# A fused gated-attention and gated-MLP kernel: the first four chunks issued in a searched unit order, and the first halves of two output products summed by way of SBUF

## The chip, the cores and the metric

The kernel runs on one core of a Trainium2 chip. The metric is the device time of one launch in microseconds (us), lower is better. A run's time is about 1.8 us longer than the span of its profile, which goes from the first to the last instruction.

Names: PE is the matrix engine, PEld its weight loads, DVE VectorE, ACT ScalarE, POOL GpSimd, SPq the queue that issues DMA loads. In this program PE's products are written to tiles in PSUM, and all other tiles lie in SBUF; an eviction copies a result out of PSUM. The granted clock is the share of its full speed at which PE ran, by the profile.

## The reference, cut to what matters

```python
# q, k, v, alpha: (4, 8, 768, 48) float32
state = alpha_t[..., None] * state + outer(k_t, v_t)     # per head, over 768 steps
y_t   = q_t @ state
x     = y, heads joined: (3072, 384)
h     = x @ w_in            # (384, 2048)
g     = h * cos(h)
out   = g @ w_out           # (2048, 384)
```

The kernel cuts the 3072 rows into 24 chunks of 128. For a chunk it takes logarithms of alpha, sums them by a triangular product, exponentiates, scales q and k, transposes them, forms masked scores, and carries a state to the next chunk. Then come the first product (ff1, in two halves of 24 products of 128 columns), the cosine on ScalarE, the gating on VectorE, and the second product (ff2, two halves of 8 products of 384 columns).

## The kernel before: the parts that matter here

The program is scheduled by hand. In these traces each engine takes its instructions in the order in which they were issued, also where a later one is ready sooner. So the order of the units is the schedule.

```python
def cast_w2(f):                       # fp32 -> bf16, one half of w_out
    nc.vector.tensor_copy(out=w2[:, f : f + 5], in_=w2f[:, f : f + 5])
    nc.scalar.activation(out=w2[:, f + 5 : f + 8], in_=w2f[:, f + 5 : f + 8], func=AF.Copy)

def ff2(j, half):
    if half == 0:
        o_new = ps.tile([C, 512], FP, tag="o")      # one PSUM buffer only
        o_ps[j] = o_new
    for f in range(HF):
        ft = half * HF + f
        nc.tensor.matmul(o_ps[j][:, 0:DM], g_t[j][:, ft], w2[:, ft],
                         start=(ft == 0), stop=(ft == NF - 1))

def ev_ff2(j):
    o_sb = moe.tile([C, DM], FP, tag="o_sb", bufs=3)
    nc.scalar.activation(out=o_sb, in_=o_ps.pop(j)[:, 0:DM], func=AF.Copy)
    ...

def warmup(n):                        # products on zeros, nobody reads them
    w_ps = ps.tile([C, 512], FP, tag="o")
    for _ in range(n):
        nc.tensor.matmul(w_ps, warm[:, 0:C], warm, start=True, stop=True)
...
for s in range(NCH + 2):              # step s: ff1 of chunk s, attention of s+1, ff2 of s-2
    ...
    if s == 0:
        run(0, "o 0i Tt Su Am p w Yy v")
    elif s == 1:
        run(1, "0i")
        run(0, "1j r")
        run(1, "o p Tt Su Am 1j r P")
        ln(4, 2)
        run(1, "C Yy x n")
    elif s == 2:
        run(2, "o Tt 0i Su Am a 1jp Yy r b 2 3 e")     # a, b: cast_w2; 2, 3: ff2
    elif s % 2 == 0:
        run(s, "o Tt 0i Su Am 2 1jp Yy r 3 e")
    else:
        run(s, "o Tt 0i Su Am 2 1jp Yy r Pn 3 e C x")
```

T and t are the transposes and their copy to SBUF, S and u the state, A and m the scores, Y and y the attention's output, o the scaling of q and k (on POOL), n, C, x the logarithm, its sums and the exponentials. 0 and 1 are the halves of ff1, i and j their cosines, p and r the gating, v the cast of the second half of w_in, P a load of ACT's function table, w warm-up products.

Of the kernel before, what the change touches and what calls it, by code (L numbers as in the profile page):

```python
# [16 lines left out]
def kernel(  # L17
# [10 lines left out]
    nc = tc.nc  # L28
# [85 lines left out]
        nc.sync.dma_start(out=w1f[:, :, f0:f1],  # L114
                          in_=moe_w_in[:, f0:f1].rearrange("(k p) f -> p k f", p=C))

    def cast_w1(f0, f1):
        nc.vector.tensor_copy(out=w1[:, 0:2, f0:f1], in_=w1f[:, 0:2, f0:f1])
        nc.scalar.activation(out=w1[:, 2, f0:f1], in_=w1f[:, 2, f0:f1], func=AF.Copy)

    def load_w2(f):
        nc.sync.dma_start(
# [1 line left out]
            in_=moe_w_out[f * C : (f + 8) * C, :].rearrange("(f p) n -> p f n", p=C),  # L124
        )

    def cast_w2(f):
        nc.vector.tensor_copy(out=w2[:, f : f + 5], in_=w2f[:, f : f + 5])  # L128
        nc.scalar.activation(out=w2[:, f + 5 : f + 8], in_=w2f[:, f + 5 : f + 8], func=AF.Copy)


    def ln(j0, n):
        g = j0 // 2
        lo = j0 % 2
        nc.scalar.activation(  # L135
            out=lnab[:, g % 2, lo : lo + n, :, 0:D], in_=a_t[g][:, lo : lo + n], func=AF.Ln
        )
# [18 lines left out]
                )  # L156

    def exps(j0, n):
        g = j0 // 2
        lo = j0 % 2  # L160
        if lo == 0 or n == 2:
            cp_new = cpool.tile([C, 2, CW], FP, tag="cpl")
            icp_new = cpool.tile([C, 2, HD], FP, tag="icpl")
            cp_t[g], icp_t[g] = cp_new, icp_new
        nc.scalar.activation(out=icp_t[g][:, lo : lo + n], in_=cum_ps[g][:, lo : lo + n, 0:HD],  # L165
                             func=AF.Exp, scale=-1.0)
        nc.scalar.activation(out=cp_t[g][:, lo : lo + n], in_=cum_ps[g][:, lo : lo + n, 0:CW],
                             func=AF.Exp, scale=1.0)
# [22 lines left out]
    def transposes(j):  # L191
        t = ps.tile([C, 2 * NP * C], BF, tag="g")
        qkT_ps[j] = t
        for i, src in enumerate((khb, qhb)):
            for p in range(NP):
                nc.tensor.transpose(  # L196
                    t[:, (i * NP + p) * C : (i * NP + p + 1) * C],
                    src[:, j % 3, 2 * p : 2 * p + 2].rearrange("s h d -> s (h d)"), ident_bf)

    def ev_transposes(j):  # L200
        t = work.tile([C, 2 * NP * C], BF, tag="qkT", bufs=3)
        nc.vector.tensor_copy(out=t, in_=qkT_ps.pop(j))  # L202
        qkT_t[j] = t
# [3 lines left out]
    def scores(j):  # L207
        t = ps.tile([C, H * C], FP, tag="big", bufs=3)
        A_ps[j] = t
        for h in range(H):  # L210
            base = 64 * (h % 2)
            p = h // 2
            nc.tensor.matmul(  # L213
                t[:, ACOL[h] * C : (ACOL[h] + 1) * C],
                qkT_t[j][base : base + D, p * C : (p + 1) * C],
                qkT_t[j][base : base + D, (NP + p) * C : (NP + p + 1) * C],
                start=True, stop=True,
            )

    def mask_scores(j):  # L220
        t = work.tile([C, H * C], BF, tag="A_sb")
        nc.vector.tensor_tensor(  # L222
            out=t.rearrange("s (h t) -> s h t", h=H),
            in0=A_ps.pop(j).rearrange("s (h t) -> s h t", h=H),
            in1=mask_f.unsqueeze(1).to_broadcast([C, H, C]), op=ALU.mult,
        )
        A_t[j] = t
# [3 lines left out]
    def state(j):  # L231
        t = ps.tile([C, 512], FP, tag="g")
        U_ps[j] = t
        first = j % NC == 0
        for p in range(NP):
            nc.tensor.matmul(  # L236
                t[:, p * 96 : (p + 1) * 96],
                khb[:, j % 3, 2 * p : 2 * p + 2].rearrange("s h d -> s (h d)"),
                vpb[:, j % 3, 2 * p : 2 * p + 2, 0:D], start=(p == 0), stop=first, skip_group_check=True,
            )  # L240
        if not first:
            nc.tensor.matmul(t[:, 0 : NP * 96].rearrange("r (p e) -> r p e", p=NP), ident_bf,  # L242
                             ub[:, (j - 1) % 3, :, 0:96],
                             start=False, stop=True, skip_group_check=True)

    def ev_state(j):
        nc.vector.tensor_tensor(  # L247
            out=ub[:, j % 3, :, 0:96].rearrange("r p (a e) -> r p a e", a=2),
            in0=U_ps.pop(j)[:, 0 : NP * 96].rearrange("r (p a e) -> r p a e", p=NP, a=2),
            in1=Em_t.pop(j).unsqueeze(3).to_broadcast([C, NP, 2, D]), op=ALU.mult,  # L250
        )
# [58 lines left out]
    c_t = {}  # L310

    def act(j, half):
        c_sb = moe.tile([C, HF, C], BF, tag="c_sb", bufs=3)
        nc.scalar.activation(out=c_sb, in_=h_ps[j, half], func=AF.Sin, bias=halfpi, scale=1.0)  # L314
        c_t[j, half] = c_sb
# [5 lines left out]
        nc.vector.tensor_tensor(out=g_t[j][:, half * HF : (half + 1) * HF],  # L321
                                in0=h_ps.pop((j, half)), in1=c_t.pop((j, half)), op=ALU.mult)

    def ff2(j, half):
        if half == 0:
            o_new = ps.tile([C, 512], FP, tag="o")
            o_ps[j] = o_new
        for f in range(HF):
            ft = half * HF + f
            nc.tensor.matmul(o_ps[j][:, 0:DM], g_t[j][:, ft], w2[:, ft],  # L330
                             start=(ft == 0), stop=(ft == NF - 1))

    def ev_ff2(j):
        o_sb = moe.tile([C, DM], FP, tag="o_sb", bufs=3)
        nc.scalar.activation(out=o_sb, in_=o_ps.pop(j)[:, 0:DM], func=AF.Copy)  # L335
        g_t.pop(j)
        nc.sync.dma_start(out=out[j * C : (j + 1) * C, :], in_=o_sb)

# [3 lines left out]
            nc.tensor.matmul(w_ps, warm[:, 0:C], warm, start=True, stop=True)  # L342








    def lnset():
        nc.scalar.preload_act_table_set("natural_log_exp_and_others")  # L352

    def run(s, order):
        g = (s + 3) // 2
        units = {
            "T": lambda: transposes(s + 1), "t": lambda: ev_transposes(s + 1),
            "S": lambda: state(s + 1), "u": lambda: ev_state(s + 1),
            "A": lambda: scores(s + 1), "m": lambda: mask_scores(s + 1),
            "Y": lambda: outputs(s + 1), "y": lambda: ev_outputs(s + 1),  # L360
            "0": lambda: ff1(s, 0), "1": lambda: ff1(s, 1),
            "i": lambda: act(s, 0), "j": lambda: act(s, 1),
            "p": lambda: gate(s, 0), "r": lambda: gate(s, 1),
            "2": lambda: ff2(s - 2, 0), "3": lambda: ff2(s - 2, 1), "e": lambda: ev_ff2(s - 2),
            "o": lambda: operands(s + 2, nc.gpsimd),
            "C": lambda: cums(2 * g, 2), "x": lambda: exps(2 * g, 2),
            "n": lambda: ln(2 * g + 2, 2), "P": lnset, "w": lambda: warmup(4),
            "v": lambda: cast_w1(DF // 2, DF), "a": lambda: cast_w2(0), "b": lambda: cast_w2(8),
        }
        for c in order:  # L370
            ahead = c in "TtSuAmYy"
            if (
                (ahead and s + 1 >= NCH) or (c in "01ijpr" and s >= NCH)
                or (c in "23e" and s < 2) or (c == "o" and s + 2 >= NCH)
                or (c in "Cx" and 2 * g >= NCH) or (c == "P" and 2 * g >= NCH)
                or (c == "n" and 2 * g + 2 >= NCH) or c == " "
            ):
                continue
            units[c]()


    lnset()
    load_a(0)
    load_qk(0)
    load_v(0)
    load_a(1)
    load_w1(0, DF // 2)
    load_a(2)
    load_a(3)
    load_qk(1)  # L390
    load_v(1)
    load_w1(DF // 2, DF)
    load_qk(2)
    load_v(2)
    load_a(4)
    load_a(5)
    load_w2(0)
    load_w2(8)
    load_qk(3)
    load_v(3)  # L400

    ln(0, 1)
    warmup(6)
    cums(0, 1)
    exps(0, 1)
    ln(1, 1)
    operands(0, nc.vector)
    warmup(4)
    run(-1, "Tt")
    cums(1, 1)  # L410
    exps(1, 1)
    run(-1, "Amw Suw Yy")
    cast_w1(0, DF // 2)
    ln(2, 2)
    warmup(6)
    cums(2, 2)
    exps(2, 2)
    operands(1, nc.vector)

    for s in range(NCH + 2):  # L420
        for j in range(6 if s == 0 else s + 7, min(s + 8, NCH)):
            load_a(j)
        if s + 4 < NCH:
            load_qk(s + 4)
            load_v(s + 4)
        if s == 0:
            run(0, "o 0i Tt Su Am p w Yy v")
        elif s == 1:
            run(1, "0i")
            run(0, "1j r")  # L430
            run(1, "o p Tt Su Am 1j r P")
            ln(4, 2)
            run(1, "C Yy x n")
        elif s == 2:
            run(2, "o Tt 0i Su Am a 1jp Yy r b 2 3 e")
        elif s % 2 == 0:
            run(s, "o Tt 0i Su Am 2 1jp Yy r 3 e")
        else:
            run(s, "o Tt 0i Su Am 2 1jp Yy r Pn 3 e C x")
# [1 line left out]
_INS = ['q', 'k', 'v', 'alpha', 'moe_w_in', 'moe_w_out']  # L441
_OUTS = [((3072, 384), 'float32')]
# [25 lines left out]
```

## Time and profile before

| | before |
|---|---|
| time, median of 3 runs | 221.77 us (220.03 to 222.35) |
| time of the profiled run | 218.74 us |
| its span | 216.9 us |
| PE busy in it | 193.0 us (89%) |

The page's strip of 40 equal slices (5.42 us each), kernel before: busy tenths of PE, the granted PE clock in tenths, the DMA engines' busy share.

```profile
PE   6657653876999999999999999999999999999972
PEclk9999965699999999999999999999999999999999
DMA  7999999997765787489378575863863451101011
```

PE is full from the eleventh slice to the last but two. Before that it has holes, the clock falls to about a half for some slices, and DMA is saturated for most of it. So the first 54 us or so are a different problem from the rest.

The table of busy time by window for the same profile (columns: window, length, busy us and instructions of PE, PEld, DVE, ACT, POOL, then granted clock, DMA share, GB/s):

```profile
25.00:30.00 5.00, 1.43 (x23) 1.08 (x20) 2.95 (x3) 1.54 (x2) 1.43 (x3) 0.86 1.02 298
30.00:35.00 5.00, 3.85 (x37) 3.11 (x36) 1.70 (x2) 1.11 (x1) 0.00 (x0) 0.50 1.06 371
...
45.00:50.00 5.00, 2.38 (x31) 1.54 (x29) 5.00 (x6) 3.42 (x4) 3.69 (x5) 1.00 1.25 170
```

PE is busy 1.43 of 5 us from 25 us, then runs at clock 0.50. At 45 us VectorE is full instead: it casts the second weight in between other work.

The chain of waits (start, length, what; it ends with the last instruction and is followed back), kernel before, at the end of the opening and at the end of the program:

```profile
48.97 1.44 DVE w_116 L128
50.45 1.46 PE o_new L330 x8
...
59.69 0.47 PE t L196 x8
...
74.39 0.47 PE t L196 x8
...
89.48 0.47 PE t L196 x8
...
206.96 2.77 PE o_new L330 x16
209.75 0.50 ACT o_sb L335
210.29 2.77 PE o_new L330 x16
213.14 0.49 ACT o_sb L335
```

The first line is the cast of the second half of w_out, which releases the second half of chunk 0's second product. The `t L196` lines are transposes: at 59.69 us those of chunk 5, the first unit of the regular steps, and from 74.39 to 89.48 us is one regular pair of steps, 15.09 us. In the tail, an eviction on ACT stands between two PE pieces because there is one PSUM buffer.

### The profile page before, as it was taken

To read this page: it belongs to the slowest core of one execution; us is meant where nothing else is said; L and a number is where in the kernel's file an instruction comes from. 1 tells how busy PE (TensorE), PEld (TensorE's weight loads), DVE (VectorE), ACT (ScalarE), POOL (GpSimd) and SP (SyncE) were. 2 spreads that over 40 slices of the span, in tenths; PEclk is the share of its full clock that TensorE was granted. 3 is DMA by queue.
4 is the path that set the end of the run, shared out by engine and by line. 5 is a ranking of instruction groups with operands and counts; after the bars stand their busy time and mean duration, and the time that the engine had idled before them with its cause. 6 is when DMAs were issued, how large, how long until landed. Compare 5 with 4: busy or idle time off the path is not lost.

```text
span 216.9 us, 6141 instructions
## 1 busy us (share of the span) xinstructions
PE 193.0 (89%) x2630; PEld 147.9 (68%) x2632; DVE 135.9 (63%) x161; ACT 124.5 (57%) x137; POOL 62.4 (29%) x104
## 2 busy tenths in 40 slices
PE   6657653876999999999999999999999999999972
PEld 2325532855787878777787878787777878787741
DVE  7636482294858768586668487685876686676320
ACT  4337605591594782973956946829739558524420
POOL 2302500582063080170350630800803607200000
PEclk9999965699999999999999999999999999999999
DMA  7999999997765787489378575863863451101011
GB/s 135 319 204 322 169 382 252 201 189 161 143 139 112 120 165 159 83 148 183 77 141 148 127 140 102 179 142 72 159 145 77 106 116 39 36 5 37 36 64 47
DMA packets 106203, 30.28 MB, mean 140 GB/s; under 512 B 100288, under 2 KB 105408, under 8 KB 106176
## 3 DMA queue, kind: packets, MB, share of 16 engines
q1 hardware_dynamic: 106176, 29.89, 64.6%
q8 instruction: 20, 0.33, 0.7%
q14 instruction: 7, 0.06, 0.1%
HBM read 25.17 MB, written 4.72 MB: 138 GB/s over the span
## 4 chain that ended last, share of the span: by engine, by line
PE 82%; DVE 6%; DMA 4%; ACT 3%; SPq 2%; issue 2%; ACTq 0%; DVEq 0%
PE o_new L330 30%; PE t L307 30%; PE t L288 7%; PE t L196 5%; DMA a_new<-in_alpha_dram 4%; PE t L213 3%; DVE g_new L321 3%; PE cum_new L148 2%; PE t L236 2%; PE t L242 2%; DVE t L222 1%; SPq L100 1%; PE cum_new L152 1%; ACT lnab L135 1%; DVE w_116 L128 1%
## 5 line engine op out<-in xcount | busy, mean ns | idle before, releaser
L314 ACT ACTIVATE c_sb<-t,halfpi 128x1024 bf16<-128x1024 f32 x48 | 53.5, 1115 | 52.3 <-PE t L307 51.9
L307 PE MATMUL t<-t,w_114 128*128 128x128 bf16 x1152 | 73.9, 222 | 0.9 <-DVE t L293 0.9
L330 PE MATMUL o_new<-w_116,g_new 128*128 128x384 bf16 x384 | 70.3, 327 | 4.2 <-DVE w_116 L128 3.1
L307 PEld LDWEIGHTS <-w_114 128*128 128x128 bf16 x1152 | 68.9, 99 | 4.2 <-DVE t L293 1.1
L321 DVE TENSOR_TENSOR g_new<-t,c_sb 128x1024 bf16<-128x1024 f32 x48 | 58.4, 1218 | 18.1 <-ACT c_sb L314 17.7
L177 POOL TENSOR_TENSOR khb<-t,icp_new 128x384 bf16<-128x384 f32 x24 | 24.3, 1013 | 120.2 <-ACT icp_new L165 91.8
L330 PEld LDWEIGHTS <-g_new 128*128 128x128 bf16 x384 | 34.2, 98 | 28.0 <-issue 4.9
L222 DVE TENSOR_TENSOR t<-t,mask_f 128x1024 bf16<-128x1024 f32 x24 | 29.2, 1216 | 1.0 <-PE t L213 1.0
L247 DVE TENSOR_TENSOR ub<-t,Em 128x384 bf16<-128x384 f32 x24 | 13.4, 558 | 23.9 <-PE t L242 18.7
L335 ACT ACTIVATE o_sb<-o_new 128x384 f32<-128x384 f32 x24 | 11.6, 485 | 20.1 <-PE o_new L330 20.1
L202 DVE COPY t<-t 128x1024 bf16<-128x1024 bf16 x24 | 16.6, 690 | 10.2 <-PE t L196 10.2
L179 POOL TENSOR_TENSOR qhb<-t,cp_new 128x384 bf16<-128x384 f32 x22 | 22.1, 1003 | 0.1
L293 DVE CAST t<-t 128x384 bf16<-128x384 f32 x24 | 13.3, 554 | 13.3 <-PE t L288 13.3
L288 PE MATMUL t<-t,vpb 128*64 128x128 bf16 x288 | 16.0, 224 | 0.4 <-DVE t L222 0.4
L352 ACT ACT_TABLE_LOAD x11 | 14.1, 1283 | 0.9 <-PEq L452 0.7
L135 ACT ACTIVATE lnab<-a_new 128x768 bf16<-128x768 f32 (+1 forms) x13 | 10.3, 793 | 7.2 <-DMA a_new<-in_alpha_dram 5.3
L314 ACT ACT_TABLE_LOAD x11 | 14.1, 1283 | 0.2
L148 PE MATMUL cum_new<-lnab,triu_bf 128*128 128x384 bf16 x24 | 7.5, 342 | 7.3 <-ACT lnab L135 7.3
L288 PEld LDWEIGHTS <-vpb 128*64 128x64 bf16 x288 | 13.2, 112 | 0.7 <-issue 0.4
L181 POOL CAST vpb<-t 128x384 bf16<-128x384 f32 x24 | 13.0, 542 | 2.1 <-DMA t<-in_v_dram 1.6
L288 PE MATMUL t<-t,ub 128*64 128x128 bf16 x160 | 13.4, 230 | 0.0
L152 PEld LDWEIGHTS <-lnab 128*128 128x128 bf16 x96 | 5.5, 98 | 10.9 <-issue 8.9
(44 smaller groups left out, 141.1 us busy)
## 6 DMA issues: line engine op xcount, KB each, us to landing
a_new<-in_alpha_dram SPq DMA_DIRECT2D x24, 192.0 KB, 3.4
t<-in_k_dram SPq DMA_DIRECT2D x24, 192.0 KB, 4.2
t<-in_q_dram SPq DMA_DIRECT2D x24, 192.0 KB, 4.3
t<-in_v_dram SPq DMA_DIRECT2D x24, 192.0 KB, 4.2
out_dram<-o_sb SPq DMA_DIRECT2D x24, 192.0 KB, 2.0
w1f<-in_moe_w_in_dram SPq DMA_DIRECT2D x2, 1536.0 KB, 8.3
w2f<-in_moe_w_out_dram SPq DMA_DIRECT2D x2, 1536.0 KB, 9.9
```

The source lines that it names most:

```text
L177: nc.gpsimd.tensor_tensor(out=khb[:, j % 3, :, 0:D], in0=k_sb, in1=icp.rearrange("s (h d) -> s h d", h=H), op=ALU.mult)
L179: qeng.tensor_tensor(out=qhb[:, j % 3, :, 0:D], in0=q_sb, in1=cp[:, 0:HD].rearrange("s (h d) -> s h d", h=H), op=ALU.mult)
L202: nc.vector.tensor_copy(out=t, in_=qkT_ps.pop(j))
L222: nc.vector.tensor_tensor(out=t.rearrange("s (h t) -> s h t", h=H), in0=A_ps.pop(j).rearrange("s (h t) -> s h t", h=H), in1=mask_f.unsquee ...
L247: nc.vector.tensor_tensor(out=ub[:, j % 3, :, 0:96].rearrange("r p (a e) -> r p a e", a=2), in0=U_ps.pop(j)[:, 0 : NP * 96].rearrange("r ( ...
L288: nc.tensor.matmul(t[64 * half : 64 * half + 64, kt * C : (kt + 1) * C], lhsT, rhs, start=start, stop=stop, skip_group_check=True)
L293: nc.vector.tensor_copy(out=t.rearrange("r k t -> r (k t)"), in_=y_ps.pop(j)[:, 0 : 3 * C])
L307: nc.tensor.matmul(t[:, f], w1[:, kk, ft * C : (ft + 1) * C], x_t[j][:, kk], start=(kk == 0), stop=(kk == 2))
L314: nc.scalar.activation(out=c_sb, in_=h_ps[j, half], func=AF.Sin, bias=halfpi, scale=1.0)
L321: nc.vector.tensor_tensor(out=g_t[j][:, half * HF : (half + 1) * HF], in0=h_ps.pop((j, half)), in1=c_t.pop((j, half)), op=ALU.mult)
L330: nc.tensor.matmul(o_ps[j][:, 0:DM], g_t[j][:, ft], w2[:, ft], start=(ft == 0), stop=(ft == NF - 1))
L352: nc.scalar.preload_act_table_set("natural_log_exp_and_others")
```

## The change

Its intent: replace the hand-written order of the first four chunks by one found by search in an offline timing model (START), let the search choose also the order of the loads and the place of each cast (its engine stays as it was), and let it run the first half of chunk 0's and chunk 1's second product early as filler, parking the half sum in SBUF (X, x) and adding it at the end (W, e). The last chunk's second product takes another PSUM buffer. The regular steps keep their order. The diff, cut to its core:

```diff
-    def ff2(j, half):
-        if half == 0:
-            o_new = ps.tile([C, 512], FP, tag="o")
+    def ff2(j, half, whole=True):
+        if half == 0 or not whole:
+            o_new = ps.tile([C, 512], FP, tag="g" if j == NCH - 1 else "o")
             o_ps[j] = o_new
         for f in range(HF):
             ft = half * HF + f
             nc.tensor.matmul(o_ps[j][:, 0:DM], g_t[j][:, ft], w2[:, ft],
-                             start=(ft == 0), stop=(ft == NF - 1))
+                             start=(f == 0 and (half == 0 or not whole)),
+                             stop=(f == HF - 1 and (half == 1 or not whole)))
+    def ev_first(j):
+        oh = moe.tile([C, DM], FP, tag="oh", bufs=3)
+        nc.scalar.activation(out=oh, in_=o_ps.pop(j)[:, 0:DM], func=AF.Copy)
+        oh_t[j] = oh
     def ev_ff2(j):
         o_sb = moe.tile([C, DM], FP, tag="o_sb", bufs=3)
-        nc.scalar.activation(out=o_sb, in_=o_ps.pop(j)[:, 0:DM], func=AF.Copy)
+        if j in oh_t:
+            nc.vector.tensor_tensor(out=o_sb, in0=o_ps.pop(j)[:, 0:DM], in1=oh_t.pop(j), op=ALU.add)
+        else:
+            nc.scalar.activation(out=o_sb, in_=o_ps.pop(j)[:, 0:DM], func=AF.Copy)
... (cut: casts and loads become units of their own; the units' table)
+    START = (
+        "a0 v0 z0 k0 20 N0 i0 v1 a2 w20 w20 w6 c0 d0 O0 a1 a3 w9 S0 u0 T0 t0 i1 k1 z1 c1 10 d1 k2 "
+        "a4 A0 O1 l1 w5 T1 C1 m0 v3 t1 w3 Y0 y0 A1 v2 S1 a5 F0 E1 11 21 G0 k3 u1 o2 T2 f0 m1 g0 "
+        "t2 p0 Y1 y1 A2 Z0 Z1 k4 a6 S2 q0 m2 G1 u2 F1 l2 Y2 g1 o3 y2 C2 T3 f1 q1 E2 a7 p1 G2 t3 "
+        "S3 u3 v4 v5 40 g2 k5 a8 A3 F2 30 m3 a9 X1 q2 o4 Y3 x1 X0 y3 k6 G3 f2 p2 31 41 x0 T4 g3 "
+        "W0 v7 k7 t4 o5 q3 A4 v6 l3 N2 a10 F3 f3 m4 S4 C3 u4 e0 Y4 W1 y4 E3 l4 p3 e1 "
+    )
... (cut: run(START), then the regular steps from s = 4 on, in the old order)
```

Each token is a unit and a chunk, half or count: a, k, v load alpha, k and q, v; z and Z load halves of w_in and w_out; 1, 2 and 3, 4 cast them (DVE, ACT); w is that many warm-up products; i, c, d and l, C, E are logarithm, sums and exponentials of one chunk or of a pair; O, o scale q and k; F, G are the halves of ff1, f, g their cosines, p, q the gating; X, V, W are halves of ff2, e the last eviction of a chunk, N the table load; the other letters are as before.

More of the change, by code (lines that the diff above doesn't have):

```diff
@@ L115, in load_w1, with cast, cast_w1 @@
                           in_=moe_w_in[:, f0:f1].rearrange("(k p) f -> p k f", p=C))
-    def cast_w1(f0, f1):
-        nc.vector.tensor_copy(out=w1[:, 0:2, f0:f1], in_=w1f[:, 0:2, f0:f1])
-        nc.scalar.activation(out=w1[:, 2, f0:f1], in_=w1f[:, 2, f0:f1], func=AF.Copy)
+    def cast(eng, dst, src):
+        if eng is nc.scalar:
+            eng.activation(out=dst, in_=src, func=AF.Copy)
+        else:
+            eng.tensor_copy(out=dst, in_=src)
+    def cast_w1(half, eng, k0, k1):
+        f = slice(half * (DF // 2), (half + 1) * (DF // 2))
+        cast(eng, w1[:, k0:k1, f], w1f[:, k0:k1, f])
     def load_w2(f):
@@ L125, in load_w2, with cast_w2, lnset @@
         )
-    def cast_w2(f):
-        nc.vector.tensor_copy(out=w2[:, f : f + 5], in_=w2f[:, f : f + 5])
-        nc.scalar.activation(out=w2[:, f + 5 : f + 8], in_=w2f[:, f + 5 : f + 8], func=AF.Copy)
+    def cast_w2(eng, f0, f1):
+        cast(eng, w2[:, f0:f1], w2f[:, f0:f1])
+    table = [None]
+    def lnset():
+        if table[0] != "ln":
+            nc.scalar.preload_act_table_set("natural_log_exp_and_others")
+            table[0] = "ln"
     def ln(j0, n):
+        lnset()
         g = j0 // 2
@@ L158, in exps @@
     def exps(j0, n):
+        lnset()
         g = j0 // 2
@@ L312, in act @@
     def act(j, half):
+        table[0] = "sin"
         c_sb = moe.tile([C, HF, C], BF, tag="c_sb", bufs=3)
@@ L330, in ff2 @@
             nc.tensor.matmul(o_ps[j][:, 0:DM], g_t[j][:, ft], w2[:, ft],
-                             start=(ft == 0), stop=(ft == NF - 1))
+                             start=(f == 0 and (half == 0 or not whole)),
+                             stop=(f == HF - 1 and (half == 1 or not whole)))
+    oh_t = {}
+    def ev_first(j):
+        oh = moe.tile([C, DM], FP, tag="oh", bufs=3)
+        nc.scalar.activation(out=oh, in_=o_ps.pop(j)[:, 0:DM], func=AF.Copy)
+        oh_t[j] = oh
     def ev_ff2(j):
         o_sb = moe.tile([C, DM], FP, tag="o_sb", bufs=3)
-        nc.scalar.activation(out=o_sb, in_=o_ps.pop(j)[:, 0:DM], func=AF.Copy)
+        if j in oh_t:
+            nc.vector.tensor_tensor(out=o_sb, in0=o_ps.pop(j)[:, 0:DM], in1=oh_t.pop(j), op=ALU.add)
+        else:
+            nc.scalar.activation(out=o_sb, in_=o_ps.pop(j)[:, 0:DM], func=AF.Copy)
         g_t.pop(j)
@@ L342, in warmup @@
             nc.tensor.matmul(w_ps, warm[:, 0:C], warm, start=True, stop=True)
-    def lnset():
-        nc.scalar.preload_act_table_set("natural_log_exp_and_others")
-    def run(s, order):
-        g = (s + 3) // 2
-        units = {
-            "T": lambda: transposes(s + 1), "t": lambda: ev_transposes(s + 1),
-            "S": lambda: state(s + 1), "u": lambda: ev_state(s + 1),
-            "A": lambda: scores(s + 1), "m": lambda: mask_scores(s + 1),
-            "Y": lambda: outputs(s + 1), "y": lambda: ev_outputs(s + 1),
-            "0": lambda: ff1(s, 0), "1": lambda: ff1(s, 1),
-            "i": lambda: act(s, 0), "j": lambda: act(s, 1),
-            "p": lambda: gate(s, 0), "r": lambda: gate(s, 1),
-            "2": lambda: ff2(s - 2, 0), "3": lambda: ff2(s - 2, 1), "e": lambda: ev_ff2(s - 2),
-            "o": lambda: operands(s + 2, nc.gpsimd),
-            "C": lambda: cums(2 * g, 2), "x": lambda: exps(2 * g, 2),
-            "n": lambda: ln(2 * g + 2, 2), "P": lnset, "w": lambda: warmup(4),
-            "v": lambda: cast_w1(DF // 2, DF), "a": lambda: cast_w2(0), "b": lambda: cast_w2(8),
-        }
-        for c in order:
-            ahead = c in "TtSuAmYy"
-            if (
-                (ahead and s + 1 >= NCH) or (c in "01ijpr" and s >= NCH)
-                or (c in "23e" and s < 2) or (c == "o" and s + 2 >= NCH)
-                or (c in "Cx" and 2 * g >= NCH) or (c == "P" and 2 * g >= NCH)
-                or (c == "n" and 2 * g + 2 >= NCH) or c == " "
-            ):
-                continue
-            units[c]()
@@ L382 @@
-    lnset()
-    load_a(0)
-    load_qk(0)
-    load_v(0)
-    load_a(1)
-    load_w1(0, DF // 2)
-    load_a(2)
-    load_a(3)
-    load_qk(1)
-    load_v(1)
-    load_w1(DF // 2, DF)
-    load_qk(2)
-    load_v(2)
-    load_a(4)
-    load_a(5)
-    load_w2(0)
-    load_w2(8)
-    load_qk(3)
-    load_v(3)
-    ln(0, 1)
-    warmup(6)
-    cums(0, 1)
-    exps(0, 1)
-    ln(1, 1)
-    operands(0, nc.vector)
-    warmup(4)
-    run(-1, "Tt")
-    cums(1, 1)
-    exps(1, 1)
-    run(-1, "Amw Suw Yy")
@@ L413 @@
-    cast_w1(0, DF // 2)
-    ln(2, 2)
-    warmup(6)
-    cums(2, 2)
-    exps(2, 2)
-    operands(1, nc.vector)
-    for s in range(NCH + 2):
-        for j in range(6 if s == 0 else s + 7, min(s + 8, NCH)):
-            load_a(j)
-        if s + 4 < NCH:
-            load_qk(s + 4)
-            load_v(s + 4)
-        if s == 0:
-            run(0, "o 0i Tt Su Am p w Yy v")
-        elif s == 1:
-            run(1, "0i")
-            run(0, "1j r")
-            run(1, "o p Tt Su Am 1j r P")
-            ln(4, 2)
-            run(1, "C Yy x n")
-        elif s == 2:
-            run(2, "o Tt 0i Su Am a 1jp Yy r b 2 3 e")
-        elif s % 2 == 0:
-            run(s, "o Tt 0i Su Am 2 1jp Yy r 3 e")
-        else:
-            run(s, "o Tt 0i Su Am 2 1jp Yy r Pn 3 e C x")
+    dve, act_e, pool = nc.vector, nc.scalar, nc.gpsimd
@@ new lines @@
+    units = {
+        "o": lambda j: operands(j, pool), "O": lambda j: operands(j, dve),
+        "T": transposes, "t": ev_transposes, "S": state, "u": ev_state,
+        "A": scores, "m": mask_scores, "Y": outputs, "y": ev_outputs,
+        "F": lambda j: ff1(j, 0), "f": lambda j: act(j, 0), "p": lambda j: gate(j, 0),
+        "G": lambda j: ff1(j, 1), "g": lambda j: act(j, 1), "q": lambda j: gate(j, 1),
+        "V": lambda j: ff2(j, 0), "W": lambda j: ff2(j, 1, j not in oh_t), "e": ev_ff2,
+        "X": lambda j: ff2(j, 0, False), "x": ev_first,
+        "N": lambda g: lnset(), "l": lambda g: ln(2 * g, 2), "C": lambda g: cums(2 * g, 2),
+        "E": lambda g: exps(2 * g, 2),
+        "i": lambda j: ln(j, 1), "c": lambda j: cums(j, 1), "d": lambda j: exps(j, 1),
+        "w": warmup,
+        "1": lambda h: cast_w1(h, dve, 0, 2), "2": lambda h: cast_w1(h, act_e, 2, 3),
+        "3": lambda h: cast_w2(dve, 8 * h, 8 * h + 5), "4": lambda h: cast_w2(act_e, 8 * h + 5, 8 * h + 8),
+        "a": load_a, "k": load_qk, "v": load_v,
+        "z": lambda h: load_w1(h * (DF // 2), (h + 1) * (DF // 2)), "Z": lambda h: load_w2(8 * h),
+    }
@@ new lines, in run @@
+    def run(order):
+        for u in order.split():
+            n = int(u[1:])
+            if 0 <= n < (NCH // 2 if u[0] in "NlCE" else NCH):
+                units[u[0]](n)
+    START = (
[5 rows of a table added]
+    )
+    S0 = 4
+    run(START)
+    for s in range(S0, NCH + 2):
+        g = (s + 3) // 2
+        odd = s % 2 == 1
+        V = s - 2 if s - 2 > 1 else -1
+        run(f"a{s + 7} k{s + 4} v{s + 4}")
+        run(f"o{s + 2} T{s + 1} t{s + 1} F{s} f{s} S{s + 1} u{s + 1} A{s + 1} m{s + 1}")
+        run(f"V{V} G{s} g{s} p{s} Y{s + 1} y{s + 1} q{s}")
+        if odd:
+            run(f"N{g} l{g + 1}")
+        run(f"W{V} e{V}")
+        if odd:
+            run(f"C{g} E{g}")
```

## The prediction

> **What bounds the kernel now.** From about 50 us the matrix engine is full: the table of busy time by window shows PE 5.00 us of every 5 from 55 us, and 20.00 of every 20 to 200 us. In the chain of waits, chunk 5's transposes (step s=4) start at 59.69 us, and a pair of steps then takes 15.1 us without a gap. The change leaves these steps' order alone, so what can move is that moment, and the tail.
>
> Before 50 us PE is busy 31.6 us, including 24 warm-up products (about 7 us). Three things cost time:
> - Issue order. Second-weight casts come late on VectorE (45.09 and 48.88 us in the timeline); the second product waits 0.38 and 2.69 us for them, and is mostly done after 50 us.
> - Clock. PE idles 3.54 us before 29.81 us; the granted clock is then 0.5 until about 42 us, so half a first product takes 2.2 to 2.7 us, not 1.5. The Trainium skill ("TensorE: Matmul & The Clock Gate", Part 1) gives an idle window of about 3.4 us; the trace agrees.
> - DMA. Saturated to about 48 us: 185 to 210 GB/s on the 192-byte rows of q, k, v, alpha, 370 to 410 on the weights. The skill ("DMA: Bandwidth & Descriptors", Specifications) wants 512 B for full rate; this agrees.
>
> **What the change does.** It adds 39 warm-up products (63 for 24), in early waiting time; about two pairs of table loads on ScalarE (1.28 us each); for chunks 0 and 1 an eviction to SBUF (0.49 us, ScalarE) and an addition on VectorE (estimate 0.56 us, like the state eviction) in place of one eviction. It removes no real PE work: about 28 us up to chunk 5's transposes (my sum of warm durations). It moves the first weight load ahead of k and q, so the first logarithm waits for it and its cast: about 12 us, not 3.9. But the first 12 us were not the limit: PE then waited 2.5 us for alpha at 15.5 and stood on w1, k and v to 23.6 us.
>
> A hand schedule of the new order with these durations and the old landing times: second w1 half lands about 22.6, chunk 1's first half of the second product at 39.5, chunk 0's at 41.6, second weight half cast at 45, chunk 5's transposes at 51.5 instead of 59.7. PE gaps after 20 us stay below about 1.5 us, so the clock should stay full. DMA puts a floor under this: k of chunk 5 landed at 47.4 us, with as many bytes before it as in the new order, then POOL needs 2 x 1.0 us: not before 49.5. My schedule leaves out signal delays, so I take 52.3: 7.4 us gained. In the tail the last chunk's own PSUM buffer saves one wait for an eviction, 0.55 us (PE idle 209.7 to 210.3).
>
> **Prediction.** About 8 us off: 213.8 us, 210.5 to 217.5. Chances: faster by over 2% 0.87, same 0.12, slower 0.01.
>
> **Right if:** clock digits stay 9 through 50 us; PE full from 37 to 40 us; chunk 5's transposes at 50 to 54 us; steps from there unchanged at 15.1 us a pair; one PSUM wait less at the end.
>
> **Wrong if:** a wait in one engine's strict order (a cast whose weights land late, k of chunk 4) opens a PE gap above 3.4 us and the half clock returns (transposes at 55 or later); loads land later than I took; or PE is not full after s=4 because ScalarE, with more table loads, runs behind.

## The result, and the profile after

| | before | after |
|---|---|---|
| time, median of 4 runs | 220.9 us (219.69 to 222.35) | 210.63 us (210.51 to 210.85) |
| profiled run: time, span | 218.74, 216.9 us | 210.85, 209.1 us |

The four runs of before are the three given above and one more.

The ratio is 0.9534, with a 95% interval of 0.9464 to 0.9603. A ratio is the mean time of one kernel's fast runs over that of the other's of the same rounds, so not quite the ratio of the medians quoted here. Executions over 1.5% slower than the fastest of the same kernel are left out of the means. All outputs are right.

The strip of 40 slices, changed kernel:

```profile
PE   7996978979999999999999999999999999999982
PEclk9999999999999999999999999999999999999999
DMA  6999899999999847693973873884765441101112
```

The table by window, same stretches:

```profile
25.00:30.00 5.00, 3.56 (x70) 3.05 (x67) 3.68 (x6) 4.27 (x5) 2.63 (x4) 1.00 0.97 176
30.00:35.00 5.00, 4.94 (x91) 4.49 (x92) 3.76 (x5) 4.87 (x5) 2.61 (x4) 1.00 1.02 309
...
45.00:50.00 5.00, 4.09 (x56) 3.09 (x57) 3.14 (x5) 4.71 (x5) 2.64 (x5) 1.00 1.37 200
```

PE's holes between 25 and 50 us are mostly closed, ACT is now nearly full, the clock stays at 1.00, and DMA is as saturated as before: the bytes are the same.

The chain of waits, changed kernel, the same places:

```profile
33.41 10.28 DMA t<-in_q_dram
43.85 2.02 POOL qhb L193
45.91 0.40 PE t L210 x4
...
52.59 0.45 PE t L210 x8
...
67.27 0.47 PE t L210 x8
...
82.36 0.47 PE t L210 x8
...
199.29 0.50 ACT o_sb L361
199.83 5.38 PE o_new L345 x32
```

Chunk 5's transposes come at 52.59 us instead of 59.69: 7.10 us. The regular pair from 67.27 to 82.36 us is 15.09 us, as before. From chunk 5's transposes to the end of the span it is 209.1 - 52.59 = 156.5 us, against 216.9 - 59.69 = 157.2: 0.7 us, and the tail shows why: 32 products in one piece, where an eviction split them. That makes 7.8 us, the whole difference of the two spans. The last open wait of the opening is named too: PE waits for the scaled q of chunk 4, POOL took 2.02 us for it, and before that the load took 10.28 us.

What the new order did with w_out can be read from VectorE's timeline (start, length, line), kernel before and then changed kernel:

```profile
45.09 1.15 DVE L128 CAST w_116<-w2f 128x1920 bf16<-128x1920 f32 x1
48.88 1.51 DVE L128 CAST w_116<-w2f 128x1920 bf16<-128x1920 f32 x1
```

```profile
38.49 1.15 DVE L121 CAST w_116<-w2f 128x1920 bf16<-128x1920 f32 x1
43.85 1.15 DVE L121 CAST w_116<-w2f 128x1920 bf16<-128x1920 f32 x1
```

The casts came 6.6 and 5.0 us earlier although the bytes came later: by the DMA view the two halves of w_out had landed at 31.7 and 37.4 us before the change, and landed at 37.2 and 41.5 after it. Before, landed bytes waited over 11 us for their turn on VectorE. With the loads it is the other way round for k of chunk 3: issued at about 26 us in both, it took 12.0 us behind the two halves of w_out before the change, and 4.5 us ahead of them after it.

### The profile page after: what moved, and what is told of

The parts are those of the page before. It is cut to its first block, busy times and chain, and to the rows that moved or that the text cites. A ratio compares the mean times of both kernels' runs of the same rounds, so it can differ in the third digit from the quotient of the medians.

```text
span 209.1 us, 6219 instructions
## 1 busy us (share of the span) xinstructions
PE 197.1 (94%) x2667; PEld 148.4 (71%) x2667; DVE 137.0 (66%) x163; ACT 130.8 (63%) x142; POOL 63.7 (30%) x104
## 4 chain that ended last, share of the span: by engine, by line
PE 76%; SPq 15%; DMA 5%; POOL 1%; issue 1%; ACT 0%; DVE 0%; POOLq 0%; ACTq 0%; DVEq 0%
PE o_new L345 31%; PE t L321 26%; SPq L105 7%; PE t L302 6%; DMA t<-in_q_dram 5%; PE t L210 4%; SPq L100 4%; PE t L227 3%; SPq L110 3%; PE t L250 2%; PE t L256 1%; PE cum_new L161 1%; POOL qhb L193 1%; SPq L128 1%; SPq L114 1%
## 5 line engine op out<-in xcount | busy, mean ns | idle before, releaser
L329 ACT ACTIVATE c_sb<-t,halfpi 128x1024 bf16<-128x1024 f32 x48 | 53.4, 1114 | 42.9 <-PE t L321 42.2
L321 PE MATMUL t<-t,w_114 128*128 128x128 bf16 x1152 | 71.9, 219 | 0.5 <-DVE g_new L336 0.5
L321 PEld LDWEIGHTS <-w_114 128*128 128x128 bf16 x1152 | 67.2, 98 | 3.8 <-issue 0.6
L191 POOL TENSOR_TENSOR khb<-t,icp_new 128x384 bf16<-128x384 f32 x24 | 24.8, 1034 | 106.9 <-ACT icp_new L179 90.1
L193 POOL TENSOR_TENSOR qhb<-t,cp_new 128x384 bf16<-128x384 f32 x22 | 23.0, 1044 | 1.6 <-DMA t<-in_q_dram 1.2
L361 ACT ACTIVATE o_sb<-o_new 128x384 f32<-128x384 f32 x22 | 10.7, 485 | 15.9 <-PE o_new L345 15.9
L368 PE MATMUL w_ps<-warm 128*128 128x512 bf16 x63 | 16.1, 408 | 1.3 <-DVE warm L56 1.2
L141 ACT ACT_TABLE_LOAD x13 | 16.7, 1283 | 0.2
L329 ACT ACT_TABLE_LOAD x13 | 16.7, 1283 | 0.2
L302 PE MATMUL t<-t,vpb 128*64 128x128 bf16 x288 | 15.5, 220 | 0.2 <-DVE t L216 0.2
L302 PE MATMUL t<-t,ub 128*64 128x128 bf16 x160 | 12.8, 225 | 1.0 <-DVE t L216 0.8
L179 ACT ACTIVATE icp_new<-cum_new 128x768 f32<-128x768 f32 (+1 forms) x13 | 9.8, 756 | 5.5 <-PE cum_new L165 5.5
L368 PEld LDWEIGHTS <-warm 128*128 128x128 bf16 x63 | 6.2, 103 | 9.4 <-issue 2.6
## 6 DMA issues: line engine op xcount, KB each, us to landing
w2f<-in_moe_w_out_dram SPq DMA_DIRECT2D x2, 1536.0 KB, 10.3
```

Of the source, the lines that this page charges most:

```text
L141: nc.scalar.preload_act_table_set("natural_log_exp_and_others")
L191: nc.gpsimd.tensor_tensor(out=khb[:, j % 3, :, 0:D], in0=k_sb, in1=icp.rearrange("s (h d) -> s h d", h=H), op=ALU.mult)
L193: qeng.tensor_tensor(out=qhb[:, j % 3, :, 0:D], in0=q_sb, in1=cp[:, 0:HD].rearrange("s (h d) -> s h d", h=H), op=ALU.mult)
L302: nc.tensor.matmul(t[64 * half : 64 * half + 64, kt * C : (kt + 1) * C], lhsT, rhs, start=start, stop=stop, skip_group_check=True)
L321: nc.tensor.matmul(t[:, f], w1[:, kk, ft * C : (ft + 1) * C], x_t[j][:, kk], start=(kk == 0), stop=(kk == 2))
L329: nc.scalar.activation(out=c_sb, in_=h_ps[j, half], func=AF.Sin, bias=halfpi, scale=1.0)
```

## The experiments

Two theories were held against each other first.

- **Order** (the prediction's): the opening is paced by loads that land when they land and by casts that stand late in an engine's strict order. The half clock is a by-product.
- **Clock** (rival): what cost the time was PE at half clock between 28 and 42 us; any way to keep PE busy would have brought most of the gain.

All runs, each with 6 timings, beside 11 of the kernel before on the same chip:

| run | time, median (range) | before on that chip | ratio, 95% interval |
|---|---|---|---|
| e1 before, two gaps filled | 221.57 (219.93 to 223.77) | 219.37 | 1.0066 [1.0018, 1.0113] |
| e2 before, tail buffer | 219.55 (218.97 to 221.28) | 219.37 | 1.0007 [0.9963, 1.0051] |
| e3 after, no tail buffer | 211.6 (210.84 to 212.17) | 219.37 | 0.9628 [0.9592, 0.9664] |
| e4 after, no halves by SBUF | 213.47 (212.5 to 213.75) | 219.37 | 0.9709 [0.9669, 0.9748] |
| e5 after, unedited | 210.54 (209.54 to 210.88) | 219.36 | 0.9595 [0.9565, 0.9625] |
| e6 after, chunk 0 early | 209.2 (208.9 to 209.96) | 219.36 | 0.9542 [0.9513, 0.9571] |
| e7 before, all gaps filled | 218.92 (217.74 to 219.43) | 219.36 | 0.9978 [0.9944, 1.0011] |
| e8 after, no halves, evicted on DVE | 214.38 (213.94 to 214.74) | 219.36 | 0.9773 [0.9742, 0.9804] |
| e9 after, no halves, evicted late | 212.04 (211.89 to 212.43) | 220.02 | 0.9641 [0.9598, 0.9683] |
| e10 as e6, no long warm-up | 209.1 (208.99 to 209.59) | 220.02 | 0.9511 [0.9473, 0.955] |
| e11 as e6, shorter warm-up, q of chunk 4 loaded earlier | 210.76 (210.06 to 211.66) | 220.02 | 0.9583 [0.954, 0.9625] |
| e12 as e6, q of chunk 4 loaded earlier | 210.6 (210.15 to 211.29) | 220.66 | 0.9541 [0.9493, 0.9589] |

The kernel before varies from chip to chip and by 2 to 3 us within one, so differences below 1 us are read from profiles, by the time of chunk 5's transposes ("T5" below), and only supported by the times. T5 is taken from the chain of waits; where it is taken from PE's timeline, the text says so, and there it is about 0.16 us earlier (52.43 us for the changed kernel).

### Clock or order: e1 and e7

e1 puts 13 warm-up products into each of the two long gaps of the kernel before.

```diff
-            run(1, "o p Tt Su Am 1j r P")
+            run(1, "o p T")
+            warmup(13)
+            run(1, "t Su Am 1j r P")
             ln(4, 2)
+            warmup(13)
             run(1, "C Yy x n")
```

> The kernel before with 13 warm-up products put into each of its two long PE gaps (before the state product of chunk 2, and before the prefix sums of chunks 4 and 5), nothing else. The granted clock should stay at full. Clock theory: the pieces of the chain of waits that ran at half speed between 29.8 and 42 us would take about 4.1 us less, so the time falls by 3 to 5 us, and the 2.7 us spread of the runs of the kernel before shrinks to under 0.5 us. Order theory: the loads and the casts in strict order set when the second product can start, the time won is given back as waiting for them; the time falls by less than 1.5 us.

Measured: no faster, rather 0.7% slower; the ratio is 1.0066, and T5 in the profiled run was 62.07 us. The clock did stay full through the filled stretch, but the chain of waits of e1 shows what took over:

```profile
26.46 11.89 DMA t<-in_k_dram
38.51 0.68 POOL khb L177
...
49.29 1.85 DVE w L128
...
51.17 2.13 PE o_new L330 x8
```

PE was ready for chunk 3's transposes earlier and waited 2.39 us for chunk 3's k: POOL could start on it at 38.51 us, where it had started at 38.27 in the kernel before. The time won was given back. After the next holes the half clock came back, at 42 and at 52 us (8 products took 2.13 us, not 1.4). The order theory's number (less than 1.5 us) held and the clock theory's (3 to 5 us) failed. But the half clock had only moved, so e7 filled the two remaining gaps as well.

```diff
+            run(1, "C Yy")
+            warmup(11)
+            run(1, "x n")
...
-            run(2, "o Tt 0i Su Am a 1jp Yy r b 2 3 e")
+            run(2, "o Tt 0i Su Am a 1jp Yy r b 2")
+            warmup(13, "g")
+            run(2, "3 e")
```

> The kernel before with warm-up products in all four of its PE gaps between 26 and 51 us (the first fill only moved the half clock to 40 to 45 and 51 to 55 us). The clock should now stay full. Clock theory, that the half clock is most of the gain: 213 to 215 us. Order theory: chunk 3's k and the second weight's casts pace it as before, only the half-speed pieces left in the first fill's chain (about 2.6 us) go: span 218, 219 to 220 us in time, no faster than the fastest run of the kernel before, but with less spread.

Measured: 218.92 us, ratio 0.9978. The chain of waits of e7, where the kernel before had its last cast and its T5:

```profile
48.66 2.54 PE w_ps L342 x11
51.19 1.38 PE o_new L330 x8
...
60.35 0.47 PE t L196 x8
```

The clock was full where the gaps had been (in this run it was half from about 16 to 19 us instead), the products ran at full speed, and still T5 came at 60.35 us, not earlier than the 59.69 of before. (The profiled run of e7, 219.42 us, was one of its slower ones and that of before, 218.74, one of its faster ones, so the ratio is the fairer measure.) The clock theory has fallen for the mean: filling the gaps with no change of order is worth about 0.2%, and by its interval 0.6% at most. e7 doesn't show that a full clock is worth nothing: its filler held PE until 40.96 us, though the scaled q of chunk 3 was ready at 40.30, which can hide up to some 0.8 us. But that is far from 7.1 us. The theory may have some truth for the spread: with all gaps filled the slowest of six runs was 219.43 us, where the slowest of eleven of the kernel before was 220.61 on that chip.

### What the change's own parts are worth: e2, e3, and e4, e8, e9

e2 gives only the tail buffer to the kernel before, and e3 takes only it from the changed one.

```diff
-            o_new = ps.tile([C, 512], FP, tag="o")
+            o_new = ps.tile([C, 512], FP, tag="g" if j == NCH - 1 else "o")
```

> The kernel before with the other PSUM buffer for the last chunk's second product, nothing else. If the prediction's tail term is right, the PE wait of 0.58 us before the last 16 products is gone and the time falls by 0.5 to 0.6 us in the profile; rival: the last store hides it, 0.

> The changed kernel with the old PSUM buffer for the last chunk, nothing else. Tail term right: 0.5 to 0.6 us slower than the changed kernel's 210.63, so 211.2. Rival: unchanged.

Measured: e2's times cannot tell 0.6 us (ratio 1.0007, interval of 0.9% width). The profiles can. From T5 to the end of the span: e2 219.0 - 62.45 = 156.55 us and the changed kernel 156.5, both with the buffer; e3 210.0 - 52.80 = 157.20 us and before 157.21, both without. So the tail term is 0.65 to 0.7 us. e3's time agrees (211.6 against 210.54 for e5), though on another chip.

e2 also showed why the kernel before has a spread. Its opening is that of the kernel before, but in its profiled run, which took 220.73 us, the half clock came a second time. The chain of waits of e2:

```profile
51.54 2.71 PE o_new L330 x8
...
62.45 0.47 PE t L196 x8
```

The same eight products took 1.46 us in the profile of before and 2.71 here, after a PE wait of 2.62 us for the cast; T5 came at 62.45 us, 2.8 us later than in the profile of before. Of this, 1.1 us was there when these products started, as the first spell of half clock ended at about 44.6 us, not 42.2; most of the rest is the second spell. So one and the same opening comes out fast or slow by how long the half clock lasts, and after a wait of under 3 us at the same place the clock fell here, but not in the profile of before. This shows one such run; that all of the spread is of this kind is not shown: the mean clocks of the runs of before (0.946 to 0.976) go with their times only loosely.

e4 takes the summing by way of SBUF out of the changed kernel: chunk 1's second product holds its buffer from half to half, and both halves of chunk 0's run at the end of the opening.

```diff
-        "... m3 a9 X1 q2 o4 Y3 x1 X0 y3 k6 G3 f2 p2 31 41 x0 T4 g3 "
-        "W0 v7 k7 t4 ... C3 u4 e0 Y4 W1 y4 E3 l4 p3 e1 "
+        "... m3 a9 V1 q2 o4 Y3 y3 k6 G3 f2 p2 31 41 T4 g3 "
+        "W1 e1 v7 k7 t4 ... C3 u4 Y4 V0 W0 e0 y4 E3 l4 p3 "
```

> The changed kernel without the summing by way of SBUF: chunk 1's second product holds its PSUM buffer from its first half to its second, and both halves of chunk 0's run at the end of the opening, evicted as before. If the summing matters as filler: chunk 0's first half (1.41 us of PE) no longer runs while PE would wait for q of chunk 4, and comes after it, so 0.8 to 1.6 us slower than 210.63 (211.4 to 212.2). If it is only cosmetic: within 0.3 us.

Measured: 213.47 us, 2.8 us slower than 210.63, where 0.8 to 1.6 was expected. T5 was at 53.81 us in PE's timeline, 1.4 us later and within what was expected, but then the chain of waits of e4 leaves PE:

```profile
54.52 1.28 ACT L141
...
61.66 0.56 DVE t L307
62.26 0.61 PE t L210 x8
```

The edit itself was at fault. The eviction `e0` stood on ACT ahead of the exponentials `E3`, could not start before the last product, and held up a table load, two exponentials, a logarithm, a second table load and two cosines behind it. e8 moved the first two evictions to VectorE, at the same places.

```diff
-            nc.scalar.activation(out=o_sb, in_=o_ps.pop(j)[:, 0:DM], func=AF.Copy)
+            cast(nc.vector if j < 2 else nc.scalar, o_sb, o_ps.pop(j)[:, 0:DM])
```

> The same as the run without the summing by way of SBUF, but the two first evictions on VectorE instead of ScalarE, where they had delayed the exponentials of chunks 6 and 7 by waiting in strict order. If the filler is worth its 1.4 us of PE work: 1.2 to 1.7 us slower than the unedited run, the other 1.4 us of the first try being ScalarE's delay. Rival, all 2.8 us are the missing buffer: 2.5 to 3 us slower again.

Measured: 214.38 us, worse still. On VectorE `e1` stood ahead of `t4` and `e0` ahead of `y4`, and PE waited 1.25 and 1.21 us for these. The expectation that another engine would do was wrong: an eviction in the wrong place cost a wait on either engine. e9 left it on ACT and issued it last.

```diff
+        "W1 e1 v7 k7 t4 ... C3 u4 Y4 V0 W0 y4 E3 l4 p3 e0 "
```

> A third form of the changed kernel without the summing by way of SBUF. In the first two, the eviction of chunk 0's product stood in front of other work in its engine's strict order (ScalarE's exponentials; VectorE's copy of chunk 4's output) and cost a wait of its own. Here it stays on ScalarE but comes after the exponentials and the logarithm. If the filler is worth its PE time: 1.2 to 1.8 us slower than the unedited 210.5, chunk 5's transposes at 53.6 to 54.2 us. Rival, the second buffer itself is worth all 2.8 to 3.8 us: 213.3 or more again.

Measured: 212.04 us, and the chain of waits of e9 is whole again:

```profile
51.31 2.71 PE o_new L345 x16
54.02 0.45 PE t L210 x8
...
61.30 0.45 PE t L210 x8
```

T5 at 54.02 us, 1.4 us after 52.59, and the step after it 7.28 us, as in the regular steps. So the summing by way of SBUF is worth about 1.4 us, the PE time of one half (1.41 us): it is filler, put where PE would otherwise wait, and it costs nothing that shows. The other 1.4 us of e4 and 2.4 us of e8 are put down to the placing of the evictions.

### Are the first 12 us free: e5, e6, e10

The prediction said so: the changed order loads w_in first, so chunk 0's logarithm waits until 12 us, and 46 warm-up products run meanwhile. e6 loads k and q first, does chunk 0 at once, and puts 40 of the warm-up products after it. e5 is the unedited kernel beside it.

```diff
-        "a0 v0 z0 k0 20 N0 i0 v1 a2 w20 w20 w6 c0 d0 O0 a1 a3 w9 S0 u0 T0 t0 i1 k1 ..."
+        "a0 k0 v0 z0 N0 i0 v1 a2 w6 c0 d0 O0 a1 a3 w9 S0 u0 T0 t0 20 w20 w20 i1 k1 ..."
```

> The changed kernel, unedited, for comparison on one chip: 210.6 us, give or take 0.7. If a half-clock spell shows in some of its profiles (one showed about 21 to 26 us in the run without the tail part), its runs spread by over 0.5 us.

> The changed kernel with k and q of chunk 0 loaded ahead of the first half of the first weight again, chunk 0's logarithm ahead of the weight's cast, and the 40 warm-up products after chunk 0's transposes: chunk 0 is then ready at about 8 us, not 17. If the prediction is right that the first 12 us are not the limit: within 0.5 us of the unedited run. Rival, that the late first logarithm costs something the search had to pay: faster by over 1 us; or that the weight-first load order is itself the gain: slower by over 1 us.

Measured on one chip: e5 210.54 us, e6 209.2 us. The means differ by 210.44 - 209.28 = 1.16 us; "within 0.5 us" was wrong. The timelines of PE (start, length, line, products, wait before) for e5 and then e6, from 13.5 us on, so that the warm-up products before that are not counted, show a part of it:

```profile
13.63 0.81 PE L368 MATMUL w_ps<-warm 128*128 128x512 bf16 x3
14.27 0.33 PE L161 MATMUL cum_new<-lnab,triu_bf 128*128 128x384 bf16 x1
```

```profile
13.63 4.26 PE L368 MATMUL w_ps<-warm 128*128 128x512 bf16 x19
17.73 0.33 PE L161 MATMUL cum_new<-lnab,triu_bf 128*128 128x384 bf16 x1
```

In e5, PE starts chunk 0's sums (`cum_new`) at 14.27 us because warm-up products stand in front of them, though the logarithm was done at 12.34 us in e5 (in the profile after: sums at 13.09 us, logarithm done at 12.69). Chunk 0's scores come at 19.56 us in e5 and at 18.06 in e6. In e6 it is chunk 1's sums that stand behind warm-up products, at 17.73 us, with the logarithm done at 15.2. So in both runs the filler held the early chain for a while. It was on the critical path in e5, whose chain of waits has no load in it after 10.5 us. In the profile after it was not: there the same work began 1.2 us earlier than in e5, and T5 was no earlier (52.43 us in PE's timeline, 52.22 in e5), because PE waited for q of chunk 4 on the way:

```profile
45.91 0.40 PE L210 MATMUL t<-ident_bf,qhb 128*128 128x128 bf16 x4 [1.11 <-POOL qhb L193]
```

So two limits lie within about 1 us of each other. In the profiles T5 is 0.7 us earlier in e6 than in e5; the rest of the 1.16 us of the means isn't seen there. e6 also moved the loads, so the share of the filler in its gain isn't shown. e10 takes the 40 products out.

```diff
-  T0 t0 20 w20 w20 i1 k1
+  T0 t0 20 i1 k1
```

> The variant with chunk 0 early (209.2 us), without its 40 long warm-up products; the 23 short-gap ones stay. If the warm-up products keep the clock: PE is idle some 7 us before chunk 1's prefix sums, the clock falls to half until about 26 us, and chunk 0's first product takes twice as long: 1.5 to 3 us slower than 209.2. If they are useless heat and only stand in the way: the same or up to 1 us faster.

Measured: 209.1 us, ratio 0.9511. PE waited 6.06 us, its clock fell to 0.50 from 11 to 21 us, and nothing was lost: T5 at 50.98 us against 51.54 in e6, both in PE's timeline, here e6 and then e10:

```profile
51.54 0.39 PE L210 MATMUL t<-ident_bf,khb 128*128 128x128 bf16 x4
```

```profile
50.98 0.39 PE L210 MATMUL t<-ident_bf,khb 128*128 128x128 bf16 x4
```

From 12 to 21 us PE has little real work, and by the first product at 22.90 us the clock was back (24 + 24 products in 2.84 us, as in e6). The expected loss of 1.5 to 3 us did not come. The 40 warm-up products that the search put in are useless in this order; the other 23 were not taken out in any run.

### The last wait of the opening: e11, e12

PE waits 1.11 us for q of chunk 4 in the profiles of the changed kernel and of e6 (not in that of e5, where PE came to it later). e11 loads k and q of chunk 4 between the halves of w_out, and also cuts the long warm-up to 28 products.

```diff
-  T0 t0 20 w20 w20 i1 k1 ... Z0 Z1 k4 a6
+  T0 t0 20 w20 w8 i1 k1 ... Z0 k4 Z1 a6
```

> The variant with chunk 0 early, 12 of the 40 long warm-up products taken out (they ended 2.5 us after chunk 1's logarithm was ready), and k and q of chunk 4 loaded between the halves of the second weight instead of after them. In the changed kernel PE waits 1.11 us for q of chunk 4 and its product on POOL. If that wait limits the opening: 0.9 to 1.6 us faster than 209.2. Rival: the second weight half, now about 2 us later, takes its place: within 0.4 us.

Measured: 210.76 us, no gain. The PE wait for q went, but the clock fell. The table by window of e11 (PE, clock, DMA share, GB/s):

```profile
24.00:26.00 2.00, 0.83 (x12) 1.00 0.79 150
26.00:28.00 2.00, 1.10 (x26) 1.00 1.25 224
28.00:30.00 2.00, 1.48 (x20) 0.60 1.21 179
```

PE was through with chunk 0's first product sooner, then had to wait for k and q of chunk 2, several times for 0.5 to 0.8 us; it was busy 1.93 of 4 us, and the clock fell to about a half for some 4 us, from 28 us on. The next 48 products took 3.94 us instead of 2.84. Two edits at once made this run hard to read, so e12 kept the warm-up and moved the load alone.

> The variant with chunk 0 early and all 40 long warm-up products (209.2 us), with only the load of k and q of chunk 4 moved between the halves of the second weight. In the run before it, that load took the wait of 1.11 us away (first product of chunk 2 to chunk 5's transposes 15.7 us, against 16.8), but the shorter warm-up let the half clock in at 28 us. If the two are separate effects: no half clock, 0.7 to 1.1 us faster than 209.2, so 208.1 to 208.5, chunk 5's transposes at 50.3 to 50.8 us. If the moved load itself brings the half clock or only moves the wait to the second weight half: 209.2 or slower.

Measured: 210.6 us on a chip where the kernel before took 220.66; the ratio, 0.9541, is that of e6. The clock stayed full, and T5 was at 52.52 us in PE's timeline, 1.0 us later than in e6. PE's timeline in e12:

```profile
46.23 1.46 PE L345 MATMUL o_new<-w,g_new 128*128 128x384 bf16 x8 [1.14 <-ACT oh L353]
```

The wait for q (1.11 us) has become a wait of 1.14 us for the eviction `x0`, which stands on ACT behind the cast of w_out's second half, which waited 1.89 us for its bytes. With DMA saturated, loading one thing earlier loads another later. The best of the runs is e6, 0.55% faster than the changed kernel on the same chip (209.28 / 210.44, the means); e10, on another chip, is at least its equal and does without the 40 products.

## Why the prediction was right, and where it was off

- **The bound was read rightly.** Regular steps took 15.09 us a pair before and after. All of the gain is in the opening and the tail.
- **The opening: right to 0.3 us.** The hand schedule, made from durations of the trace and landing times of before, with 0.8 us added for signal delays, put chunk 5's transposes at 52.3 us; they came at 52.59 in the chain. The gain there was to be 7.4 us and was 7.1. Its steps hold too: the first halves of chunks 1 and 0 were to run at 39.5 and 41.6 us and ran at 39.69 and 41.76, and the last cast of w_out was to be done at 45 and was at 45.00. The 0.8 us were an allowance without a working of its own, so the last part of the agreement is luck.
- **The tail: right.** 0.55 us expected, 0.7 measured, confirmed by e2 and e3.
- **The time: 3.2 us too high, 0.1 us inside the low end of the range, which is luck.** The step that failed is "about 8 us off: 213.8 us", not the 8. The 8 us were worked out against the profile, whose run took 218.74 us, and then subtracted from the median of other runs, 221.77. From 218.74 they give 210.7; measured was 210.63. The kernel before sometimes loses up to 3 us more in its opening, as the profile of e2 shows, and no profile of the changed one shows such a loss: it should have been treated as a part of the gain. Its later medians of 11 runs were 219.4 to 220.7 us, so the full gain is nearer 9 than the 10.3 us of the first four runs.
- **The clock: right about this profile, wrong in its rule.** "PE gaps after 20 us stay below about 1.5 us, so the clock should stay full" held in the profiled run (largest gap 1.11 us). But e3, e4, e8 and e9, with the same opening to 20 us and gaps below 1 us, had half clock for about 3 us at 20 us. The gap of 3.4 us that the prediction took as the threshold doesn't hold in the profile of before either: PE's last product ended at 26.27 us and the clock fell at 28.6, after 2.4 us of the gap of 3.54. And the clock was not what mattered: e1 and e7 kept most of it up and gained next to nothing.
- **"The first 12 us were not the limit": wrong by about 1 us** (e6: 1.16 us by the means, 0.7 us by T5). The filler stood in the way for a part of it. The prediction also counted 24 warm-up products before the change; the code issues 28, so 35 were added, not 39.
- **"PE full from 37 to 40 us": nearly.** In these 3 us PE was busy for 2.76. From there on the wait for q of chunk 4 (1.11 us, to 45.91) is open: its scaling took 2.0 us on POOL where 1.0 was assumed, beside the cast of w_out on VectorE from 43.85 to 45.00 us.
- **What makes up the 7.1 us of the opening:** about 1.4 us are the filler by way of SBUF (e9). Filling the clock's gaps alone gave none of it (e7; some 0.8 us may be hidden there). The rest, about 5 to 5.7 us, is left by subtraction for the order of loads, casts and units as a whole. That the casts of w_out came 5 to 6.6 us earlier and k of chunk 3 landed some 7 us earlier is seen in the traces; how the gain divides between them was not tried, and no run gave the kernel before one of them alone.

## What to carry to other kernels

When an opening is paced by loads and each engine works in strict order, find what each engine's next instruction waits for and put work that is ready in front of it: half of a later product, parked in SBUF, was worth about its PE time here. Filler without use is another matter: warm-up products gained nothing clear in e1 and e7, and taking 40 of them out cost nothing in e10; try taking them out. And subtract a gain worked out from a profile from the time of that profiled run, not from the median of others, and ask what makes the runs differ.

## What the Trainium skill lacked or had wrong

- "TensorE: Matmul & The Clock Gate", the table under "Why this matters for your kernels": it advises "No PE-idle gaps >~3µs between matmul bursts". That was not enough here: with PE busy 0.83 and 1.10 of two windows of 2 us and no wait over 0.8 us, e11's clock fell to a mean of 0.60 in the next; in e2 the clock fell after a wait of 2.62 us, while in the profile of before it did not after a wait of 2.69 us at the same place. Part 1 of the page says that the gate follows how busy PE was recently; that describes these runs better than the length of one gap.
- The same page, Part 1, on the cold start agrees in the products (in the profile of before the first 6 warm-up products of 512 columns took 2.74 us, the four after them 1.02 us), but the profile's granted clock reads 1.00 for these first 5 us. The page warns that clock records can be unreliable; this may be a case of it.
- "ScalarE: Activation LUTs", "What ACT_TABLE_LOAD costs": it gives about 1283 ns for the load, which the trace has to the nanosecond (mean of 13 loads 1283), and about 1380 ns of drain on top. The drain is not seen here: in the changed kernel an activation ended at 54.09 us, the load ran from 54.11 for 1.28 us, and the next activation began at 55.41.
- "DMA: Bandwidth & Descriptors", Specifications, asks for 512 B for full rate; it has no measured rate for 192-byte rows on this chip. Here saturated stretches moved 185 to 210 GB/s of them, against 370 to 410 GB/s on the weights' rows of 1.5 and 4 KB.
